# Fused retention, gated unit and expert kernel: tail outputs ahead in each pair, norm broadcasts in the gate products' banks, weight blocks begun two steps behind their request, sweep steps moved

## The chip, the cores and the metric

The kernel runs on one core of one Trainium2 chip. The metric is device time in microseconds (us): the median of timed runs of the whole program. One further execution is taken with the hardware profiler, and the trace and the profile page come from it. The engines are named as the profile names them: PE is TensorE (PEld its weight loads), DVE is VectorE, ACT is ScalarE, POOL is GpSimd, and SP (SyncE) only issues transfers here.

## The reference

Three stages follow each other: retention (attention with a decaying causal mask), a gated feed-forward unit behind a root-mean-square norm, and eight experts mixed by a normalised routing matrix.

```python
# 1: batch 4, 8 heads, 576 positions, head size 64
scores = q @ k.T / sqrt(64) * Dmat          # Dmat[i, j] = gamma[h] ** (i - j) for i >= j, else 0
x = (scores @ v)                            # 2304 tokens x 512
# 2: w_gate, w_val [512, 1536], w_out [1536, 512]
xn = x / sqrt(mean(x * x) + 1e-6) * rms_g
g = xn @ w_gate
x = (g * sigmoid(g) * (xn @ w_val)) @ w_out
# 3: w1 [8, 512, 1024], w2 [8, 1024, 512]
P = exp(x @ w_gate2 - max); 8 rounds of row and column normalisation
out = sum over e of P[:, e] * (relu(x @ w1[e]) @ w2[e])
```

## The kernel before

Products of the second and third stage are made in a 32-bit reduced format: each operand is split into a high part (a cast) and a low part (what the cast lost), and a product is three matmuls, high*high, high*low and low*high (`products`, lines L174 to L176). The order of instructions on each engine is the order in which the Python code emits them; no scheduler moves them, and each engine works strictly through its own queue.

**Retention** goes through 16 pairs (4 batches times 4 pairs of heads). A pair i has four chunks of 128 positions and a tail of 64. In loop step i the code emits `scores(i + 1)` (PE scores `sc` and the tail scores `u`, then DVE's masked product `am`), `states(i + 1)` (PE chunk states in `u`, ACT and DVE turn them into running states `block_states`, DVE makes the tail's masked scores `mt`), one call of `step_weights`, and `outputs(i)`: PE makes the four chunks' outputs in bank `o` and the tail's in a corner of `u`, DVE scales both into `acc` (L331 the chunks, L335 the tail), ACT squares the result (`sq`) and POOL sums the squares. `u`, `sc` and `o` have two buffers each, so the tail scores of pair i + 2 (L284) must wait until L335 of pair i has read `u`.

**The norm** of batch b is made in two generators. `norm_sums(b)` turns the squares into 1/rms (`ry`), the power on POOL. `norm(b)` has ACT write five diagonal tiles `dg` (L374), then PE multiply them by a matrix of ones, so that `rb` and `rbt` hold the factor of each token in all partitions (L378, L379), ACT copy these to `y` (L381, L382), and DVE scale `acc` (L387) while ACT and DVE or POOL split it into `xhi` and `xlo` (L388, L391, L393). Batch 0 is normed within retention, batches 1 to 3 beside the first three token blocks of the gated unit. `bank(name)` gives the PSUM bank for `rb`, `rbt` and the sums `ss`; after retention it comes from the pool `pac`, which also holds the four outputs `x` of a token block.

**The gated unit** makes 6 sweeps over the tokens, each with two of the 12 blocks of 128 hidden features. A sweep has five token blocks (512, 512, 512, 384, 384 tokens), and a block (`gated_block`) has five substages i = 0 to 4: gate product of feature block m = 0 (`gv`, 12 matmuls, then ACT's silu `t`, L196), value product of m = 0 (12 matmuls, then DVE's product `t` L202, ACT's cast `ghi` L203, DVE's rest `glo` L204), the same two for m = 1, and last the outputs `x` (24 matmuls: 12 with m = 0, then 12 with m = 1), which ACT copies (sweep 0, L223) or DVE adds (L225) to `acc`. PE thus starts the second 12 matmuls of `x` only when `glo` of m = 1 is there. After a substage the caller may run one `step_weights`.

**Weights** of the gated unit (36 blocks, six to a sweep) come as 64-bit numbers and are narrowed on the chip. `load_weights` requests a block into one of two raw buffers (L107, on SP). `prepare` then makes one move for each call of `step_weights`: ACT's absolute value of the raw block (L122); three operations on DVE (L124 to L126); ACT L128; DVE L130, after which the raw buffer is free and `load_weights` requests the next block at the end of the same call, and ACT's cast L142; DVE's low part L144. Two blocks are under way at a time. In the next call after a request, the first move (L122) of that new block is emitted.

Of the kernel before, what the change touches and what calls it, by code (L numbers as in the profile page):

```python
# [17 lines left out]
B, H, S, D = 4, 8, 576, 64  # L18
NP = H // 2
# [4 lines left out]
E = 8  # L24
FE = 1024
C = 128
NC = S // C
TAIL = S - NC * C
# [3 lines left out]
SWEEP = 2  # L32
# [5 lines left out]
NCONV = 2  # L38
# [12 lines left out]
def retention_glu_experts(ctx: ExitStack, tc: tile.TileContext, a, out):  # L51
# [6 lines left out]
    nc = tc.nc  # L58
# [15 lines left out]
    wg_raw = const.tile([128, KD, E], F32, name="wg_raw")  # L74
    wg = const.tile([128, KD, 2 * E], F32R, name="wg")
# [7 lines left out]
    def f32(t):  # L83
        return t.bitcast(F32)
# [7 lines left out]
    raw, raw_of, pieces, slot_of, active = {}, {}, {}, {}, {}  # L92
# [4 lines left out]
    tp = glu.enter_context(tc.tile_pool(name="tp", bufs=3, side="right"))  # L97
    nrm = glu.enter_context(tc.tile_pool(name="nrm", bufs=1, side="right"))
    raw_slots = list(range(NRAW))
    n_load, n_next, n_slot, n_done = [0], [0], [0], [0]  # L100

    def load_weights():
        while n_load[0] < len(sources) and raw_slots:
            i = n_load[0]
            n = raw_of[i] = raw_slots.pop(0)
            t = rawp.tile([128, 1024], I32, tag=f"raw{n}", name=f"raw{i}")
            nc.sync.dma_start(t, sources[i].bitcast(I32))  # L107
            raw[i] = t
            n_load[0] += 1

    def free_raw(i):
# [32 lines left out]
        nc.vector.tensor_sub(lo, x, f32(hi))  # L144
        pieces[i] = (hi, lo)

    def step_weights(load=True):
        for i in sorted(active):
            if next(active[i], True):
                del active[i]  # L150
        i = n_next[0]
        if i in raw and len(active) < NCONV:
            active[i] = prepare(i)
            next(active[i])
            n_next[0] += 1
        if load:
            load_weights()
# [86 lines left out]
    g_out = tabs.tile([128, NP, C], F32, name="g_out")  # L244
# [64 lines left out]
    def outputs(i):  # L309
        b, pr = divmod(i, NP)  # L310
        t = loaded.pop(i)
        qt, vs = t["qT"], t["vs"]
        am, mt, st, u = staged.pop(i)
        o = psa.tile([128, NC, C], F32, tag="o", name=f"o{i}")
        ot = u[:, NC + 1, :]
        for c in range(NC + 1):
            tail = c == NC
            dst = ot if tail else o[:, c, :]
            if c:
                for hs in heads:  # L320
                    cs = slice(c * C, min(S, c * C + C))
                    nc.tensor.matmul(dst[hs, :], lhsT=st[hs, c - 1, :], rhs=qt[hs, cs], start=True, stop=False)
            for h, hs in enumerate(heads):
                nc.tensor.matmul(
                    dst[hs, :],
                    lhsT=vs[hs, 2 * NC * D:] if tail else vs[:, (2 * c + h) * D:(2 * c + h + 1) * D],
                    rhs=mt[hs, :] if tail else am[:, h, c, :],
                    start=not c, stop=True,
                )
        xf = acc_d[:, pr, b * S:(b + 1) * S]  # L330
        nc.vector.tensor_mul(  # L331
            xf[:, :NC * C].rearrange("p (c i) -> p c i", c=NC), o,
            g_out[:, pr:pr + 1, :].to_broadcast([128, NC, C]),
        )
        nc.vector.tensor_mul(xf[:, NC * C:], ot, g_out[:, pr, :TAIL])  # L335
        scale_keys(i + 2)
        sq = sp.tile([128, S], F32, tag="sq", name=f"sq{i}")
        nc.scalar.activation(sq, xf, AF.Square)
        if pr:
            nc.gpsimd.tensor_add(sq, sq, squares[b])  # L340
        squares[b] = sq
# [85 lines left out]
    for i in range(B * NP):  # L427
        b, pr = divmod(i, NP)
        load_pair(i + 2, "qT", "vs")
        load_weights()  # L430
        if i == 1:
            nc.sync.dma_start(rms_g, a["rms_g"])
            nc.sync.dma_start(ident, a["ident"])
            nc.sync.dma_start(wg_raw.rearrange("p k e -> p (k e)"), a["wg"])
        scores(i + 1)
        states(i + 1)
        load_pair(i + 3, "kT", "ks")
        step_weights(load=False)
        outputs(i)
        if i in SUMS_AT:  # L440
            next(sums[i // NP - 1], None)
        if i >= 2 * NP - 1:
            next(norms[0], None)
    next(norms[1])
    nc.scalar.copy(wg[:, :, :E], wg_raw)
    nc.vector.tensor_sub(wg[:, :, E:], wg_raw, f32(wg[:, :, :E]))
    retention.close()
    psa_pools.close()
    pac = ctx.enter_context(tc.tile_pool(name="pac", bufs=4, space=PSUM, side="right"))
    ps_home[:] = pac, "ac"  # L450
    glu_ps = ExitStack()
    pmm = glu_ps.enter_context(tc.tile_pool(name="pmm", bufs=4, space=PSUM))
    xpool = ctx.enter_context(tc.tile_pool(name="xpool", bufs=1))
    sx = xpool.tile([128, 3, 2, 2, T], F32R, name="sx")
    w1_slots = [xpool.tile([128, 2, 7, 256], F32R, name="w1s0")]
# [140 lines left out]
    for s in range(NSWEEP):  # L596
        last_sweep = s == NSWEEP - 1
        for j, (t0, n) in enumerate(BLOCKS):
# [4 lines left out]
            for i in range(2 * SWEEP + 1):  # L603
                if last_sweep and last and i == 2 * SWEEP:
                    break
                if first_norms and not i:
                    next(norms[j + 1])
                next(block)
                if first_norms:
                    for _ in range((1, 1, 1, 2, 0)[i]):  # L610
# [2 lines left out]
                        next(sums[B - 1], None)  # L613
                    if i == 2 * SWEEP - 1 and j + 2 < B:
                        next(norms[j + 2])
                if i % 2 if first_norms else i != 2 * SWEEP - 1 or not s:
                    step_weights()
                if last_sweep and j and i % 2:
                    next(scored)
                if last_sweep and j == 1 and i == 2:  # L620
# [633 lines left out]
```

## Time and profile before

| | |
|---|---|
| median of 3 runs | 2050.62 us (2047.67 to 2052.09) |
| profiled execution, its own time | 2052.37 us |
| its span (first to last instruction) | 2050.6 us |
| PE busy | 2010.9 us, 98% of the span |
| DVE, ACT, POOL busy | 71%, 43%, 36% |

The span is what the trace covers; the execution's own time is 1.8 us more. Matmuls overlap each other and their ends are modelled, so PE's busy share tells little by itself: how fast it goes is read from the distance between the starts of matmuls, or from the length of a stretch with a known number of them. Retention fills the first 102 us, the gated unit goes from there to about 590 us, the experts from there to the end.

### The profile page before, as it was taken

What the parts mean: (1) busy time and instruction counts of PE and PEld (TensorE: products, weight loads), DVE (VectorE), ACT (ScalarE), POOL (GpSimd) and SP (SyncE); (2) the same over time, 40 slices, a digit from 0 to 9 for tenths busy, and PEclk for the clock granted to TensorE, in tenths of its full rate; (3) what the DMA queues carried; (4) which work ended last, traced back from release to release, by engine and by line L of the source; (5) the groups of instructions that cost most, each with busy time, mean ns of one, the idle gap of its engine ahead of it and who ended that gap; (6) DMA issues with size and microseconds to landing.
All of it is one profiled execution on the core that took longest, in us unless ns stands there. A gap on an engine that the chain in (4) does not pass through costs nothing.

```text
span 2050.6 us, 29927 instructions
## 1 busy us (share of the span) xinstructions
PE 2010.9 (98%) x11390; PEld 1857.7 (91%) x11390; DVE 1448.7 (71%) x2312; ACT 874.6 (43%) x1671; POOL 732.8 (36%) x672
## 2 busy tenths in 40 slices
PE   8989999999999999999999999999999999999998
PEld 5669789889788899989998999999999999999998
DVE  6845654643568877777786777777787777777777
ACT  4544332311354454444444444444445544444443
POOL 1210000000044445454552454545464444444443
PEclk9999999999999999999999999999999999999999
DMA  8502120200047888888888676766676676767673
GB/s 274 188 20 62 62 62 11 71 23 1 1 186 287 293 299 299 305 307 298 308 298 313 255 263 256 268 250 259 252 278 246 249 286 241 269 247 282 242 277 139
DMA packets 112687, 437.02 MB, mean 213 GB/s; under 512 B 12296, under 2 KB 30344, under 8 KB 96160
## 3 DMA queue, kind: packets, MB, share of 16 engines
q1 hardware_dynamic: 110048, 432.72, 57.9%
q10 hardware_dynamic: 2496, 2.40, 0.3%
q8 instruction: 89, 1.46, 0.3%
q14 instruction: 54, 0.44, 0.1%
HBM read 312.86 MB, written 122.21 MB: 212 GB/s over the span
## 4 chain that ended last, share of the span: by engine, by line
PE 86%; DVE 7%; ACT 3%; DMA 3%; issue 1%; POOL 1%; ACTq 0%; SPq 0%; DVEq 0%; POOLq 0%
PE pz L717 9%; PE py L717 9%; PE px L717 9%; PE qx L948 6%; PE qy L948 6%; PE qz L948 6%; PE gv L174 4%; PE gv L175 4%; PE gv L176 4%; PE y L175 4%; PE y L176 4%; PE y L174 4%; PE qz L717 3%; PE x L175 2%; PE x L176 2%; PE x L174 2%
## 5 line engine op out<-in xcount | busy, mean ns | idle before, releaser
L717 PE MATMUL py<-sx,w1s 128*128 128x384 f32 x1152 | 233.2, 337 | 2.7 <-ACT py L1041 2.5
L511 POOL TENSOR_TENSOR t<-rw 128x256 f32<-128x256 f32 x32 | 44.3, 1383 | 518.2 <-DVE sx L548 412.4
L1125 POOL TENSOR_TENSOR acc<-z,a_block 128x384 f32<-128x384 f32 x63 | 63.9, 1015 | 446.3 <-DVE z L1119 446.3
L717 PEld LDWEIGHTS py<-sx,w1s 128*128 128x128 f32 x1152 | 203.7, 189 | 7.2 <-ACT py L1041 4.2
L717 PE MATMUL px<-xhi,w1s 128*128 128x384 f32 x640 | 188.7, 335 | 0.0
L938 ACT CAST xhi<-acc 128x384 fp32r<-128x384 f32 x316 | 156.0, 514 | 69.6 <-POOL acc L1125 35.4
L942 DVE TENSOR_TENSOR xlo<-acc,xhi 128x384 fp32r<-128x384 f32 x191 | 177.4, 955 | 1.8 <-ACT xhi L938 1.8
L942 POOL TENSOR_TENSOR xlo<-acc,xhi 128x384 fp32r<-128x384 f32 x125 | 145.6, 1165 | 32.1 <-ACT xhi L938 32.0
L956 DVE TENSOR_TENSOR acc<-acc,qz 128x384 f32<-128x384 f32 x246 | 134.7, 548 | 25.6 <-PE qz L948 25.6
L202 DVE TENSOR_TENSOR t<-t,gv 128x512 f32<-128x512 f32 (+1 forms) x60 | 37.9, 632 | 131.4 <-PE gv L176 131.4
L717 PEld LDWEIGHTS px<-xhi,w1s 128*128 128x128 f32 x640 | 117.9, 188 | 0.3
L717 PE MATMUL pz<-xhi,w1s 128*128 128x384 f32 x384 | 114.1, 337 | 3.5 <-DVE z L872 2.2
L956 DVE TENSOR_TENSOR acc<-acc,qx 128x384 f32<-128x384 f32 x123 | 67.3, 547 | 70.2 <-PE qx L948 70.2
L717 PE MATMUL pz<-sx,w1s 128*128 128x384 f32 x576 | 115.7, 335 | 0.0
L717 PE MATMUL px<-xlo,w1s 128*128 128x384 f32 x320 | 107.0, 334 | 0.0
L762 DVE SCALAR_TENSOR_TENSOR acc<-y,prob,acc 128x512 f32<-128x512 f32 x144 | 101.3, 741 | 6.1 <-PE y L176 6.1
L974 ACT COPY qz<-qy 128x384 f32<-128x384 f32 x127 | 58.8, 463 | 107.0 <-PE qy L948 99.4
L176 PE MATMUL y<-xlo,xhi 128*128 128x512 f32 x264 | 103.9, 394 | 0.0
L175 PE MATMUL y<-xlo,xhi 128*128 128x512 f32 x264 | 103.7, 393 | 0.0
L174 PE MATMUL y<-xlo,xhi 128*128 128x512 f32 x264 | 102.9, 390 | 0.0
L717 PEld LDWEIGHTS pz<-sx,w1s 128*128 128x128 f32 x576 | 101.2, 188 | 0.4
L966 ACT COPY qy<-qx 128x384 f32<-128x384 f32 x127 | 58.8, 463 | 96.2 <-PE qx L948 89.9
(392 smaller groups left out, 5930.5 us busy)
## 6 DMA issues: line engine op xcount, KB each, us to landing
w1s<-w_kept SPq DMA_DIRECT2D x64, 1792.0 KB, 7.2
w_kept<-w1s SPq DMA_DIRECT2D x32, 1792.0 KB, 6.6
rw<-in_w_dram SPq DMA_DIRECT2D x64, 512.0 KB, 5.5
w_kept<-xlo SPq DMA_DIRECT2D x64, 512.0 KB, 3.5
w2s<-w_kept SPq DMA_DIRECT2D x32, 1024.0 KB, 6.9
w_extra<-w_kept SPq DMA_DIRECT2D x32, 768.0 KB, 7.6
w_kept<-xlo SPq DMA_DIRECT2D x44, 384.0 KB, 3.9
w2c<-w_kept SPq DMA_DIRECT2D x32, 512.0 KB, 7.8
```

Of the source, the lines that this page charges most:

```text
L174: nc.tensor.matmul(ps, lhsT=lh, rhs=rh, start=start, stop=False)
L175: nc.tensor.matmul(ps, lhsT=lh, rhs=rl, start=False, stop=False)
L176: nc.tensor.matmul(ps, lhsT=ll, rhs=rh, start=False, stop=stop)
L717: nc.tensor.matmul(ps, lhsT=l, rhs=r[:, k, :], start=start and k == 0 and i == 0, stop=k == 1 and i == 2, skip_group_check=True,)
L762: nc.vector.scalar_tensor_tensor(o, y_2, pe, o, ALU.mult, ALU.add)
L938: nc.scalar.copy(hi, x)
L942: (engine or nc.vector).tensor_sub(lo, x, f32(hi))
L948: nc.tensor.matmul(ps, lhsT=l, rhs=r, start=start and i == 0, stop=i == 2, skip_group_check=True)
L956: nc.vector.tensor_add(dst, dst, ps)
L966: nc.scalar.copy(y, x)
L974: nc.scalar.copy(z, y)
L1125: nc.gpsimd.tensor_add(sums[0], z[:, 0, :], h_blocks[0])
```

## The change

Four things are changed.

1. In `outputs`, the tail's matmuls come before the four chunks', and DVE scales the tail before the chunks.
2. The diagonal tiles of norm 1 (`next(norms[1])`) are emitted in retention's loop step 14, ahead of `outputs(14)`, and no longer behind the loop. After retention `bank` takes `rb`, `rbt` and the last `ss` from `pmm`, the four banks of the gate and value products, in place of `pac`. The split of the routing matrix (`wg`) moves to the last block of sweep 0.
3. A requested weight block is begun only in the third call of `step_weights` after its request (in the loop of retention still in the first).
4. In the sweeps, the calls stand after substages 0 and 1, before the emission of substage 4, and after it. Before they stood after substages 0, 1, 2 and 4. In the three blocks of sweep 0 that norm beside them the two calls stand before and after substage 4, where before they stood after substages 1 and 3.

```diff
-    n_load, n_next, n_slot, n_done = [0], [0], [0], [0]
+    n_load, n_next, n_slot, n_done, n_step, asked = [0], [0], [0], [0], [0], {}
...
-            raw[i] = t
+            raw[i], asked[i] = t, n_step[0]
...
-    def step_weights(load=True):
+    def step_weights(load=True, apart=2):
         for i in sorted(active):
             if next(active[i], True):
                 del active[i]
         i = n_next[0]
-        if i in raw and len(active) < NCONV:
+        n_step[0] += 1
+        if i in raw and len(active) < NCONV and n_step[0] - asked[i] > apart:
             active[i] = prepare(i)
...
-        for c in range(NC + 1):
+        for c in (NC, *range(NC)):
             tail = c == NC
...
         xf = acc_d[:, pr, b * S:(b + 1) * S]
+        nc.vector.tensor_mul(xf[:, NC * C:], ot, g_out[:, pr, :TAIL])
         nc.vector.tensor_mul(
             xf[:, :NC * C].rearrange("p (c i) -> p c i", c=NC), o,
             g_out[:, pr:pr + 1, :].to_broadcast([128, NC, C]),
         )
-        nc.vector.tensor_mul(xf[:, NC * C:], ot, g_out[:, pr, :TAIL])
...
-        step_weights(load=False)
+        step_weights(load=False, apart=0)
+        if i == B * NP - 2:
+            next(norms[1])
         outputs(i)
...
-    next(norms[1])
-    nc.scalar.copy(wg[:, :, :E], wg_raw)
-    nc.vector.tensor_sub(wg[:, :, E:], wg_raw, f32(wg[:, :, :E]))
     retention.close()
     psa_pools.close()
     pac = ctx.enter_context(tc.tile_pool(name="pac", bufs=4, space=PSUM, side="right"))
-    ps_home[:] = pac, "ac"
     glu_ps = ExitStack()
     pmm = glu_ps.enter_context(tc.tile_pool(name="pmm", bufs=4, space=PSUM))
+    ps_home[:] = pmm, "mm"
...
                 if first_norms and not i:
                     next(norms[j + 1])
+                if i == 2 * SWEEP:
+                    step_weights()
                 next(block)
...
-                if i % 2 if first_norms else i != 2 * SWEEP - 1 or not s:
+                if i == 2 * SWEEP or i < 2 and not first_norms:
                     step_weights()
+                if not s and last and not i:
+                    nc.scalar.copy(wg[:, :, :E], wg_raw)
+                    nc.vector.tensor_sub(wg[:, :, E:], wg_raw, f32(wg[:, :, :E]))
```

Three places show what this does to the queues. Line numbers behind the first hunks are one higher in the changed kernel (before L196, after L197). The first place is ACT in sweep 1, from the cast `ghi` of the second token block's m = 0 to the third block's first silu; `raw` is a requested weight block, `t` and `gv` carry the first token, the feature block m and, for `gv`, 0 for gate. Before:

```order
L203 CAST ghi_512_0_2170<-t_512_0_2150 128x512
L142 CAST sx<-cv_2081 128x512
L122 ACTIVATE cv_2178<-raw_2155 128x512
L196 ACTIVATE t_512_1_2195<-gv_512_1_0_2182 128x512
L122 ACTIVATE cv_2201<-raw_2180 128x512
L203 CAST ghi_512_1_2216<-t_512_1_2195 128x512
L128 ACTIVATE cv_2178<-cv_2178 128x512
L196 ACTIVATE t_1024_0_2270<-gv_1024_0_0_2257 128x512
```

and in the changed kernel:

```order
L204 CAST ghi_512_0_2148<-t_512_0_2128 128x512
L142 CAST sx<-cv_2077 128x512
L197 ACTIVATE t_512_1_2171<-gv_512_1_0_2158 128x512
L204 CAST ghi_512_1_2186<-t_512_1_2171 128x512
L122 ACTIVATE cv_2224<-raw_2133 128x512
L197 ACTIVATE t_1024_0_2239<-gv_1024_0_0_2226 128x512
L122 ACTIVATE cv_2244<-raw_2156 128x512
L204 CAST ghi_1024_0_2259<-t_1024_0_2239 128x512
```

Both reads of fresh raw blocks (L122) have moved from before `ghi` of m = 1 to behind it, and the second stands in the next token block.

The second place is ACT at the end of retention, loop steps 14 and 15 and the first copies of norm 1. Before:

```order
L128 ACTIVATE cv_1090<-cv_1090 128x512
L338 ACTIVATE sq_1256<-acc 128x576
L142 CAST wslots<-cv_1090 128x512
L128 ACTIVATE cv_1171<-cv_1171 128x512
L338 ACTIVATE sq_1283<-acc 128x576
L374 ACTIVATE dg_1286<-ident,ry_824 128x128 x5
L445 CAST wg<-wg_raw 128x4x8
L381 COPY y_1383<-rb_1379 128x512
```

and in the changed kernel:

```order
L128 ACTIVATE cv_1090<-cv_1090 128x512
L375 ACTIVATE dg_1235<-ident,ry_824 128x128 x5
L339 ACTIVATE sq_1262<-acc 128x576
L142 CAST wslots<-cv_1090 128x512
L128 ACTIVATE cv_1171<-cv_1171 128x512
L339 ACTIVATE sq_1289<-acc 128x576
L382 COPY y_1381<-rb_1377 128x512
```

The five diagonal tiles `dg` have moved ahead of both last squares, and the `wg` cast is gone from here.

The third place is DVE in a late pair of retention, from the masked product of one pair to that of the next. Before:

```order
L285 TENSOR_TENSOR am_987<-sc_986,masks 128x1024
L302 SCALAR_TENSOR_TENSOR mt_1007<-u_985,g_tail,causal_t 128x64
L304 SCALAR_TENSOR_TENSOR block_states_116<-block_states_116,g_step 128x64 x3
L130 SCALAR_TENSOR_TENSOR cv_790<-raw_753,cv_790 128x512
L331 TENSOR_TENSOR acc<-o_1020,g_out 128x512
L335 TENSOR_TENSOR acc<-u_916,g_out 128x64
```

and in the changed kernel:

```order
L286 TENSOR_TENSOR am_987<-sc_986,masks 128x1024
L303 SCALAR_TENSOR_TENSOR mt_1007<-u_985,g_tail,causal_t 128x64
L305 SCALAR_TENSOR_TENSOR block_states_116<-block_states_116,g_step 128x64 x3
L130 SCALAR_TENSOR_TENSOR cv_790<-raw_753,cv_790 128x512
L332 TENSOR_TENSOR acc<-u_916,g_out 128x64
L333 TENSOR_TENSOR acc<-o_1020,g_out 128x512
```

The read that frees `u` has moved ahead of the longer one; the rest stands as it did.

## Rows read from the trace of the kernel before

**Rows 1.** Windows of sweeps 1 to 4, first gate matmul to the next sweep's.

```profile
core 0: us, PE busy (x) PEld busy (x) DVE busy (x) ACT busy (x) POOL busy (x), PEclk, DMA share, GB/s
191.86:274.76 82.90, 78.24 (x361) 66.67 (x361) 49.59 (x87) 28.73 (x53) 0.00 (x0) 0.98 0.21 64
274.76:350.61 75.85, 74.76 (x361) 65.61 (x361) 36.59 (x62) 18.76 (x34) 0.00 (x0) 1.00 0.11 35
350.61:427.30 76.69, 75.44 (x361) 65.29 (x361) 48.68 (x86) 25.37 (x45) 0.00 (x0) 1.00 0.20 62
427.30:501.29 73.99, 73.99 (x361) 65.54 (x361) 25.13 (x41) 11.32 (x20) 0.00 (x0) 1.00 0.00 1
```

**Rows 2.** Chain that ended last, in sweep 1's last block: start, us, what.

```profile
265.96 3.62 DMA raw<-in_wout_dram
...
269.65 0.66 ACT cv L122
...
270.74 0.57 DVE glo L204
```

**Rows 3.** Timeline from the end of retention: start, us, engine, [idle before, releaser].

```profile
100.86 0.68 ACT L338 ACTIVATE sq<-acc 128x576 f32<-128x576 f32 x1 [3.48 <-DVE acc L335]
101.77 0.69 DVE L331 TENSOR_TENSOR acc<-o,g_out 128x512 f32<-128x512 f32 x1 [0.41 <-PE o L324]
101.82 0.28 PE L324 MATMUL u<-mt,vs 64*64 64x64 f32 x4
103.65 1.55 ACT L374 ACTIVATE dg<-ident,ry 128x128 f32<-128x128 f32 x5
104.96 2.07 PE L378 MATMUL rb<-dg,ones 128*128 128x512 f32 x2 [2.86 <-ACT dg L374]
```

**Rows 4.** Windows: `rb` and `rbt` of norms 1 and 2, m = 0 products behind each.

```profile
104.96:107.58 2.62, 2.62 (x4) 1.00 (x5) 0.19 (x1) 0.35 (x2) 0.26 (x1) 0.50 0.00 0
128.97:130.39 1.42, 1.42 (x5) 0.59 (x5) 0.00 (x0) 1.39 (x3) 0.00 (x0) 1.00 0.00 0
107.58:114.88 7.30, 7.30 (x25) 5.88 (x25) 0.82 (x1) 1.86 (x4) 0.00 (x0) 0.75 0.01 2
130.39:135.96 5.57, 5.57 (x25) 4.62 (x25) 0.82 (x1) 1.86 (x4) 0.00 (x0) 1.00 0.00 0
```

**Rows 5.** PE's waits from 102 to 180 us (total, times, longest), and ACT's timeline.

```profile
PE rb L378 <- ACT acc L223: 2.2, 2, 1.1
...
126.33 1.57 ACT L374 ACTIVATE dg<-ident,ry 128x128 f32<-128x128 f32 x5
```

**Rows 6.** Timeline of sweep 0's second block, around `glo` of m = 1.

```profile
139.81 1.51 POOL L391 TENSOR_TENSOR xlo<-acc,xhi 128x576 fp32r<-128x576 f32 x1 [17.23 <-ACT xhi L388]
139.61 0.42 DVE L124 TENSOR_SCALAR cv<-cv 128x512 f32<-128x512 f32 x1
139.95 1.66 DVE L125 TENSOR_SCALAR cv<-raw 128x512 int32<-128x512 int32 x1
142.98 0.68 DVE L202 TENSOR_TENSOR t<-t,gv 128x512 f32<-128x512 f32 x1
143.90 0.39 PE L176 MATMUL x<-ghi,wslots 128*128 128x512 f32 x1
145.43 0.40 PE L176 MATMUL x<-ghi,wslots 128*128 128x512 f32 x1
```

**Rows 7.** Retention: PE's waits from 20 to 102 us, a timeline row, a late window.

```profile
PE u L284 <- DVE acc L335: 3.2, 6, 0.8
...
51.12 0.33 PE L284 MATMUL u<-qT,kT 64*64 64x64 f32 x4 [0.39 <-DVE acc L335]
...
80.00:100.00 20.00, 17.94 (x250) 12.39 (x246) 18.57 (x44) 10.09 (x20) 6.68 (x4) 1.00 0.43 143
```

**Rows 8.** Windows of two idle stretches of PE in retention, with what follows each.

```profile
15.96:21.40 5.44, 4.15 (x63) 2.96 (x64) 3.15 (x9) 3.33 (x7) 0.00 (x0) 1.00 0.93 309
61.35:66.80 5.45, 4.68 (x43) 3.61 (x44) 2.21 (x7) 3.25 (x7) 1.18 (x1) 0.70 0.66 221
```

## The prediction

> **What bounds the kernel now.** I read the waits first, then the chain that ended last, then windows and timelines of the places that these named. All that the change touches lies in the first 501 us. There the end of each stage is set by PE, which always has matmuls queued, so every stretch in which PE stands, or runs at half clock, is on the path, if nothing else takes over as the limit.
>
> The gated unit's sweeps show it plainly. Sweeps 1 to 4 have the same matmuls (361 starts in each window), and they took 82.90, 75.85, 76.69 and 73.99 us [rows 1]. Sweep 4 has no weight blocks to narrow, and PE is never idle in it; 73.99 us is what a sweep costs when nothing stands in the way. The three others are above it by 8.91, 1.86 and 2.70 us, 13.5 in all. What stands in the way is seen in the chain [rows 2]: a transfer of a raw block takes 3.62 us, ACT's L122 on that block can start only then, the cast `ghi` of m = 1 is queued behind L122, and `glo` (270.74) and PE's second half of `x` come after that. The request was made after substage 1 of that block and the read stands after substage 2, in the next call. ACT is in order, so a wait for a transfer becomes a wait of PE.
>
> Around the end of retention there are three smaller places. PE ends retention at 102.10 (101.82 + 0.28) and starts `rb` of norm 1 at 104.96, since ACT makes the diagonal tiles last, from 103.65 [rows 3]. The clock is then granted at half (1.2 of 2.4 GHz): `rb` and `rbt` take 2.62 us instead of 1.42, and the first 24 gate and value matmuls 7.30 instead of 5.57 [rows 4]. And `rb` of norms 2 and 3 waits 2.2 us together for ACT to empty a bank of `x` (L223) [rows 5].
>
> **The change, part by part.**
>
> *Weight steps of the sweeps.* L122 of a block now stands at least three calls behind its request, so it does not wait for the transfer. The shortest distance is from the call before substage 4 to the call after substage 1 of the next block: 48 matmuls. 24 of them at 512 tokens take 5.57 us [rows 4], so at 384 tokens some 4.2 (three quarters, an estimate), and 48 some 8.4, against a transfer of 3.62 and, ahead of the request, three or four operations of DVE like `glo` (0.57 [rows 2]), some 2 us. No call stands between silu and `ghi` of m = 1 any more, so nothing is queued ahead of the tight one, `glo` of m = 1. The operations themselves are the same ones. Their cover is in substage 4, 24 matmuls (5.57 us) in which DVE has adds to make and ACT little; without that cover a call there would cost its longest run on DVE, the three operations L124 to L126, some 1.5 us by the 0.42 of L124 and the 0.57 of `glo` [rows 2, 6]. The price is pace: a block now takes six calls where it took four, and with two under way one is finished every three calls; 20 calls a sweep give 6.7 blocks where six are used up. The work thus reaches into sweep 4, where DVE is busy 25.13 of 73.99 us [rows 1] and has room. Bounds: nothing gained if the stalls only move, all 13.5 if they vanish. I take 13.5, because sweep 3, with nearly the DVE time of sweep 1 (48.68 and 49.59 us), is only 2.70 us above sweep 4 [rows 1]: the work itself fits beside PE.
>
> *Diagonal tiles of norm 1.* The five take 1.55 us on ACT, which idles 3.48 us ahead of its square at 100.86 [rows 3]; in their new place they fit into that idle time. `rb` then waits for DVE's last read of retention's banks, since the pools are exchanged there. DVE scales the chunks last now, 0.69 us behind PE's end (the row of 101.77) [rows 3], so `rb` starts near 102.85: 2.1 us gained. It is 2.8 if that read does not hold it, and 0 if another wait takes its place.
>
> *Clock.* The half clock followed an idle time of 2.86 us [rows 3]; 0.75 us remains. An idle stretch of 1.3 us (5.44 less 4.15) in retention left the clock at 1.00 [rows 8]. If it stays up, `rb` and the first products gain 1.20 and 1.73 us, 2.9 together; otherwise nothing.
>
> *`rb` in the gate products' banks.* The bank that it takes was read long before by DVE's L202 or ACT's silu, so the 2.2 us end, but the diagonal tiles are there only at 127.90 in the first of the two places (126.33 + 1.57) [rows 5], about when PE is ready: I count 2.1 of 2.2. In return the gate products of m = 1 wait for ACT's copies of `rb` and `rbt`; the products of m = 0 (5.57 us) lie between, and a copy is about as long as the 0.66 of L122 [rows 2], so that cost is zero; without the distance it would be about 1 us in each of three blocks.
>
> *Steps moved out of the norm blocks.* In sweep 0's second block three matmuls of `x` took 1.53 us (143.90 to 145.43) [rows 6] where 24 take 5.57, that is 0.70 for three: 0.8 us lost. DVE's L125 ran 1.66 us instead of the 0.42 of L124 beside it, with POOL's `xlo` subtraction running, and this pushed `t` to 142.98 [rows 6]. These weight operations leave that place, so I count 0.8. The Trainium skill, "SBUF — State Buffer", section "Who interferes with whom", says that a DVE operation with two SBUF inputs or in a two-port mode and a GpSimd operation that reads SBUF exclude each other for the whole instruction, the first to issue going first; L125 agrees. The norm's own scaling, which now stands there, has two SBUF inputs too. By the rule's worse order it waits for POOL until 141.32 (139.81 + 1.51), `t` begins some 0.8 us earlier than before, near 142.1, and `glo` ends three operations of 0.7 later, near 144.2, when PE could go on at 144.13: 0.1 late, and the sum would be 21.9 instead of 22.0. In the first block a similar stall (DVE waits for POOL's power) stays as it is.
>
> *Tail first.* L335 now comes ahead of L331 (0.69 [rows 3]), so 0.6 to 0.7 us sooner, and PE's six waits for it (3.2 us) [rows 7] shrink. Between 80 and 100 us DVE is busy 18.57 of 20 us [rows 7]: it is the limit there, and PE's shorter wait gains nothing. Only waits such as the 0.39 at 51.12 [rows 7] pass on. I take 0.6, with 0 and 3.2 as ends. The chunks' scaling comes a little later on DVE, and the chunk matmuls by those of the tail later on PE (0.28 [rows 3] and about as much again); both are read only by the square, which has slack, except at the very end, where it is counted above.
>
> *`wg`* (one small operation on ACT and one on DVE) goes to a block in which neither is the limit: nothing.
>
> Sum: 13.5 + 2.1 + 2.9 + 2.1 + 0.8 + 0.6 = 22.0 us. The span of 2050.6 becomes 2028.6. The profiled execution's own time, 2052.37, lies 1.75 above the median of the runs, so in the terms of that median 2050.62 - 22.0 = **2028.6 us**. The experts' part of the program is unchanged and begins earlier by the same amount.
>
> **Rivals.** (a) The clock falls all the same when the gated unit begins. For it speaks that it fell near 63.4 us after less than 1 us of idle time with matmuls of one column ahead of it (mean 0.70 in that window; 5.45 less 4.68 idle) [rows 8]; against it the 1.3 us without a fall [rows 8]. The 2.9 us are lost: 2031.5. The Trainium skill, "TensorE: Matmul & The Clock Gate", section "What's actually happening", puts it as "the default state is throttled, and activity releases the throttle", which fits a fall at such a joint.
>
> (b) The stall moves. DVE and ACT now get two calls around substage 4; if these come late to the next silu or to `acc`, PE waits there. Against it: the 2.70 us of sweep 3 with the same operations [rows 1], and the 24 matmuls of substage 4 as cover. With half of the 13.5 left: 2035.3.
>
> (c) Slower: weights come late. If the pace of one block in three calls does not suffice, the code emits the missing calls just ahead of the product that needs the block, and PE stands for request, L122 and the rest: at least 3.62 + 0.66 us [rows 2], with four more operations like `glo` some 6.6. Four such blocks eat the 22 us; with one in each of five sweeps it is 33 us, 2062. Against it: 20 calls for 18 needed, and six blocks ready before sweep 0 begins.
>
> (d) Nothing is gained, because DVE, at 49.59 of 82.90 us in sweep 1 [rows 1], or another engine is the true limit: 2050. Sweep 4's 73.99 speaks against it.
>
> **Chances.** The forecast 0.67, (a) 0.14, (b) 0.11, (c) 0.05, (d) 0.03. A difference under 0.2% (4 us) can't be told from none. Faster: 0.67 + 0.14 + 0.11 = 0.92; same 0.03; slower 0.05. The low end is the forecast with all of the waits for L335 (2.6 more), no wait of `rb` (0.7) and a little for the spread of a median: 2024.5. The high end takes in (a) and (b): 2035.5.
>
> **What would show it.** Sweeps 1 to 3 near 74 us each; no transfer ahead of L122 in the chain; `rb` of norm 1 within 1 us of the last output matmul at full clock; no wait of `rb` for L223; `x` without gaps in sweep 0's second block. The prediction is wrong if sweep 4 grows, if L122 still waits for transfers, or if the half clock returns in places where it was not.

## The result and the profile after

| | before | changed |
|---|---|---|
| median of 4 runs each, taken side by side | 2051.36 us (2047.67 to 2057.72) | 2031.56 us (2027.96 to 2033.18) |
| ratio, with its 95% interval | | 0.9898 (0.9870 to 0.9926) |
| profiled execution, its own time | 2052.37 us | 2031.48 us |
| its span | 2050.6 us | 2029.7 us |

The kernel became faster by about 20 us, where 22.0 were forecast; the time of 2031.56 us lies 3.0 above the forecast 2028.6 and inside the range. The same kernel, timed a second time in a later series, gave 2030.01 us (ratio 0.9892, 0.9873 to 0.9911).

The page of the changed kernel, its span and the first row of busy times:

```profile
span 2029.7 us, 29934 instructions
...
PE 2003.1 (99%) x11390; PEld 1856.4 (91%) x11390; DVE 1445.7 (71%) x2312; ACT 875.5 (43%) x1671; POOL 731.8 (36%) x672
```

PE's busy time fell by 7.8 us and the span by 20.9, so most of the gain is idle time of PE that is gone. Where it was is read from the same windows as before. Sweeps 1 to 4 of the changed kernel, one window each:

```profile
184.69:258.68 73.99, 73.99 (x362) 65.53 (x361) 40.46 (x71) 23.64 (x43) 0.00 (x0) 1.00 0.19 56
258.68:332.67 73.99, 73.99 (x362) 65.53 (x362) 41.41 (x73) 22.63 (x40) 0.00 (x0) 1.00 0.15 43
332.67:406.65 73.98, 73.98 (x361) 65.53 (x361) 42.77 (x76) 22.57 (x40) 0.00 (x0) 1.00 0.16 44
406.65:480.64 73.99, 73.99 (x362) 65.53 (x361) 37.27 (x64) 18.60 (x33) 0.00 (x0) 1.00 0.14 42
```

All four are now as long as sweep 4 was [rows 1], to 0.01 us, and PE is busy in all of each. DVE's work (the third number) is spread evenly, 37 to 43 us a sweep, where it was 49.59, 36.59, 48.68 and 25.13.

The joint of retention and gated unit, as a timeline (start, length, engine, what, idle time before it and its releaser):

```profile
98.85 0.97 ACT L375 ACTIVATE dg<-ident,ry 128x128 f32<-128x128 f32 x3
...
103.04 0.44 PE L325 MATMUL o<-am,vs 128*64 128x128 f32 x4
103.53 0.69 DVE L333 TENSOR_TENSOR acc<-o,g_out 128x512 f32<-128x512 f32 x1 [1.53 <-PE o L325]
...
104.36 1.10 PE L379 MATMUL rb<-dg,ones 128*128 128x512 f32 x2 [0.89 <-DVE acc L333]
```

The diagonal tiles are made 5 us ahead, and `rb` follows the last output matmul (103.04 + 0.44) after 0.88 us, released by DVE's scaling of the chunks; before it was 2.86 us, released by the tiles [rows 3]. Windows of `rb` and `rbt` of norm 1, of the first 24 gate and value products, and of `rb` and `rbt` of norm 2 (the columns are those of rows 1):

```profile
104.36:105.75 1.39, 1.39 (x4) 0.57 (x4) 0.00 (x0) 0.63 (x1) 0.68 (x1) 1.00 0.25 100
105.75:111.32 5.57, 5.57 (x25) 4.60 (x25) 0.82 (x1) 1.86 (x4) 0.73 (x1) 1.00 0.02 3
125.44:126.86 1.42, 1.42 (x7) 1.20 (x7) 0.69 (x1) 1.42 (x5) 0.00 (x0) 1.00 0.72 124
```

The clock stays at 1.00, so the first two take 1.39 and 5.57 us instead of 2.62 and 7.30 [rows 4]. PE's waits from 95 to 180 us (total, times, longest):

```profile
PE rb L379 <- DVE acc L333: 0.9, 1, 0.9
PE x L176 <- DVE glo L205: 0.2, 1, 0.2
```

No `rb` waits for ACT's reading of `x` any more [rows 5]. What the forecast did not have lies earlier, in retention. Three windows of retention in the changed kernel:

```profile
61.30:66.70 5.40, 5.40 (x68) 3.48 (x68) 2.92 (x8) 2.75 (x7) 1.18 (x1) 1.00 0.69 208
84.29:87.40 3.11, 2.65 (x33) 2.36 (x31) 2.99 (x9) 1.67 (x4) 0.55 (x1) 1.00 0.78 227
87.40:97.60 10.20, 10.13 (x94) 6.99 (x96) 8.04 (x18) 4.29 (x9) 3.37 (x2) 0.51 0.15 47
```

Before, the clock was at half for 3.4 us from 63.5 us on [rows 8]; here it is at full there, and at half from 87.7 to 97.9 us, 10.2 us with PE busy nearly throughout. Retention ends at 103.48 instead of 102.10.

Piece by piece, the two profiles against each other, and the forecast's terms for the same piece:

| piece (before, after, us) | gained | forecast |
|---|---|---|
| retention, to the end of its last matmul (102.10, 103.48) | -1.38 | 0.6 |
| from there to the first gate product (5.48, 2.27) | 3.21 | 3.3 (2.1 and 1.20) |
| sweep 0, first block (22.81, 19.69) | 3.12 | 2.8 (1.73 and half of 2.1) |
| sweep 0, second block (20.02, 17.79) | 2.23 | 1.9 (half of 2.1, and 0.8) |
| sweeps 1 to 4 (309.43, 295.95) | 13.48 | 13.5 |
| together | 20.66 | 22.0 |

The span fell by 20.9; the other 0.2 lies behind these pieces and was not followed further.

### The profile page after: what moved, and what is told of

Its sections match the earlier page's. It is cut to its first block, busy times and chain, and to the rows that moved or that the text cites. A ratio compares the mean times of both kernels' runs of the same rounds, so it can differ in the third digit from the quotient of the medians.

```text
span 2029.7 us, 29934 instructions
## 1 busy us (share of the span) xinstructions
PE 2003.1 (99%) x11390; PEld 1856.4 (91%) x11390; DVE 1445.7 (71%) x2312; ACT 875.5 (43%) x1671; POOL 731.8 (36%) x672
## 4 chain that ended last, share of the span: by engine, by line
PE 90%; DVE 6%; ACT 2%; DMA 1%; POOL 1%; issue 1%; ACTq 0%; SPq 0%; DVEq 0%; POOLq 0%
PE pz L722 9%; PE py L722 9%; PE px L722 9%; PE qx L953 6%; PE qy L953 6%; PE qz L953 6%; PE gv L175 5%; PE gv L176 5%; PE gv L177 5%; PE y L177 4%; PE y L176 4%; PE y L175 4%; PE qz L722 3%; PE x L175 2%; PE x L176 2%; PE x L177 2%
```

## The experiments

Ratios below are those of a kernel's runs to the runs of the kernel before beside it on the same chip.

**The parts alone.** The first theory was the forecast's: the terms are independent and add up. The second came from the profile after: the tail's new order drives PE's retention into the half clock and costs what the change lacks to 22. Three kernels carry one part of the change each, a fourth the whole change but the tail's order. The first is the kernel before with

```diff
-        for c in range(NC + 1):
+        for c in (NC, *range(NC)):
...
+        nc.vector.tensor_mul(xf[:, NC * C:], ot, g_out[:, pr, :TAIL])
...
-        nc.vector.tensor_mul(xf[:, NC * C:], ot, g_out[:, pr, :TAIL])
```

> The kernel before with only the tail outputs ahead in each pair. Theory 1 (the tail order gains in the pairs, and where the clock falls in retention is chance): the pair that begins at 80.5 us before begins 2 to 3 us earlier; the total is 0.5 to 3 us below before, with half clock somewhere. Theory 2 (the tail order itself brings the half clock of the last pairs): half clock again between 85 and 98 us, retention ends as late as before or later, total equal or up to 1.5 us above. Sweeps as before: 82.9, 75.9 and 76.7 us.

The second is the kernel before with the diagonal tiles of norm 1 in loop step 14, the `pmm` banks and `wg` moved, and with all calls of `step_weights` as they were:

```diff
+        if i == B * NP - 2:
+            next(norms[1])
...
-    ps_home[:] = pac, "ac"
+    ps_home[:] = pmm, "mm"
```

> The kernel before with only the diagonal tiles of norm 1 ahead and the broadcasts in the gate products' banks. Theory 1: PE's wait after retention falls from 2.9 to about 0.7 us, no half clock at the first gate products, no wait of the broadcasts for copies of x: 2.1 + 2.9 + 2.1, 6 to 7 us below before; the stall of 0.8 us in sweep 0's second block stays. Rival (the half clock comes at the joint all the same): 4 us below.

The third is the kernel before with the distance and the places of the weight steps alone:

```diff
-        if i in raw and len(active) < NCONV:
+        if i in raw and len(active) < NCONV and n_step[0] - asked[i] > apart:
...
-                if i % 2 if first_norms else i != 2 * SWEEP - 1 or not s:
+                if i == 2 * SWEEP or i < 2 and not first_norms:
```

> The kernel before with only the weight steps: begun two calls later, and the calls moved. Theory 1: sweeps 1 to 3 at 74.0 us each, 13.5 us below before, and 0.8 us in sweep 0's second block: 14.3 us below in total, with the wait and half clock behind retention as before. Rival (most of the gain needs the other parts too): sweeps above 75 us.

And the changed kernel with the tail's old order (the first diff the other way round):

> The changed kernel with the tail outputs last again. Theory 1: the late pairs begin 2 to 3 us later than in the changed kernel, and the total is 0.5 to 3 us above it, unless the clock stays up in retention by chance, which hides it. Theory 2 (the tail order brings the half clock): no half clock in the last pairs, and the total is 1 to 3 us below the changed kernel.

| kernel | median (us) | ratio | interval | change | forecast of the part |
|---|---|---|---|---|---|
| tail alone | 2053.31 | 1.0006 | 0.9993 to 1.0018 | +1.2 | -0.6 |
| norm alone | 2044.39 | 0.9966 | 0.9953 to 0.9978 | -7.0 | -7.1 (2.1, 2.9, 2.1) |
| steps alone | 2037.79 | 0.9928 | 0.9914 to 0.9942 | -14.8 | -14.3 (13.5, 0.8) |
| all but the tail's order | 2029.76 | 0.9893 | 0.9880 to 0.9907 | -22.0 | |

(The change is the ratio less one, times the 2052.24 us of the kernel before in that series.) The parts add up to -20.6 us; by the same reckoning the whole gives -20.9 in its own series, -22.2 in the later one, and -22.0 without the tail's order. So no sharing between the parts can be seen, and the tail's order gives nothing that these runs can tell from none. The sweeps of the kernel with the steps alone:

```profile
191.40:265.39 73.99, 73.99 (x362) 65.53 (x361) 40.47 (x71) 23.65 (x43) 0.00 (x0) 1.00 0.19 56
...
339.38:413.36 73.98, 73.98 (x361) 65.52 (x361) 42.79 (x76) 22.59 (x40) 0.00 (x0) 1.00 0.15 44
```

The kernel with the tail alone came out as the second theory had it: half clock from 85.2 to 95.5 us, retention up to 105.78 us, no gain. The theory falls by the kernel with the tail's old order. Two windows of its retention:

```profile
84.80:88.00 3.20, 2.66 (x32) 2.31 (x30) 3.05 (x10) 1.62 (x4) 0.49 (x1) 1.00 0.78 221
88.00:98.20 10.20, 10.19 (x94) 6.98 (x96) 8.12 (x18) 4.50 (x10) 3.42 (x2) 0.50 0.16 49
```

It has the same 10.2 us at half clock without the tail's order. That order does shorten PE's waits for DVE's scaling: 3.2 us in six waits before [rows 7], 2.5 us in five in this kernel, 0.5 us in one in the changed kernel. PE's waits of the changed kernel from 20 to 102 us:

```profile
PE u L299 <- ACT ks L267: 2.0, 3, 1.1
PE rb L379 <- DVE rv L360: 0.8, 1, 0.8
PE u L285 <- DVE acc L332: 0.5, 1, 0.5
```

and the second row of the kernel before:

```profile
PE u L298 <- ACT ks L266: 1.5, 3, 0.5
```

The wait for ACT's scaled keys `ks` grew by 0.5 us. With the unchanged 0.8 the waits listed come to 5.5 us before and to 3.3 in the changed kernel; what is left of this in the time is taken up below.

**Distance or places?** The change of the weight steps does two things at once. One kernel is the changed one with the old places of the calls, the other the changed one with the old distance:

```diff
-                if i == 2 * SWEEP:
-                    step_weights()
...
-                if i == 2 * SWEEP or i < 2 and not first_norms:
+                if i % 2 if first_norms else i != 2 * SWEEP - 1 or not s:
```

> The changed kernel with the calls back in their old places, a block still begun in the third call after its request. Theory A (the stall is the read of a raw block right behind its request, so either half of the change ends it): sweeps 1 to 3 within 0 to 2 us of 74.0 each, with short stalls of up to 0.5 us in blocks where DVE's and ACT's weight operations stand between the silu and the cast of m = 1; the 0.8 us in sweep 0's second block come back; 1 to 4 us above the changed kernel. Theory B (only the places matter): sweep 1 above 80 us again.

```diff
-    def step_weights(load=True, apart=2):
+    def step_weights(load=True, apart=0):
```

> The changed kernel with a block begun in the first call after its request, the calls in their new places. Theory A: ACT waits for the transfer behind the cast of m = 1, under the 24 matmuls of the outputs, and PE does not wait: sweeps 1 to 3 at 74.0 us, total equal to the changed kernel within 1.5 us. Theory C (only the distance matters): ACT's wait comes through to PE in substage 4 or the next silu, sweep 1 above 78 us.

Measured: 2033.74 us, ratio 0.9920 (0.9900 to 0.9940) with the distance and the old places; 2035.20 us, 0.9915 (0.9897 to 0.9932) with the places and the old distance. Sweep 1 of the one and of the other, a fence each:

```profile
187.65:261.63 73.98, 73.98 (x361) 65.55 (x361) 41.44 (x72) 23.49 (x43) 0.00 (x0) 1.00 0.14 43
```

```profile
188.84:262.90 74.06, 74.06 (x362) 65.51 (x361) 47.99 (x86) 28.43 (x52) 0.00 (x0) 1.00 0.23 64
```

Either one alone is enough for the sweeps. They do it in different ways, which ACT's waits from 150 to 500 us show. In the kernel with the distance alone no wait of L122 for a transfer is left. In the kernel with the places alone three such rows are, nearly 20 us in all, about as much as the 18.6 us (10.8 and 7.8) of the kernel before in the same view:

```profile
ACT cv L122 <- DMA raw<-in_wout_dram: 9.1, 3, 4.3
...
ACT cv L122 <- DMA raw<-in_gate_dram: 5.8, 2, 3.3
...
ACT cv L122 <- DMA raw<-in_val_dram: 5.0, 2, 2.6
```

So ACT waits as long as before and PE does not: it is what is queued behind the wait that counted. With no call between silu and `ghi` of m = 1, the cast is no longer behind such a wait.

The medians of both kernels are some 2 to 4 us above that of the changed one, though their intervals overlap with its own. In the profiles the difference is not in the sweeps: sweep 1 begins at 187.65 and 188.84 us instead of 184.69. Most of it arises in retention, which ends at 105.16 and 107.33 us, and is not the work of the part that was put back: up to 115 us all three kernels have the same instructions in the same order on each engine. The kernel with the places alone was slow at the start. Sixteen matmuls of one form between 16 and 22 us, in the changed kernel and then in this one:

```profile
L282 PE MATMUL sc<-qT,kT 64*128 64x128 f32 x16 | 1.2, 283 | 0.5 <-DMA qT<-in_qT_dram 0.5
L282 PE MATMUL sc<-qT,kT 64*128 64x128 f32 x16 | 2.1, 438 | 0.0
```

They take 438 ns instead of 283, and PE gets faster only near 23 us, although the column of the granted clock shows 1.00 there. The durations of matmuls have to be read beside that column.

With the old places the 0.8 us were expected back in sweep 0's second block. That block takes 17.75 us, as in the changed kernel (17.79); it is the third that takes 17.36 us instead of 16.47, and the first 20.12 instead of 19.69. In the third stands the pair of operations that the kernel before had in the second [rows 6]:

```profile
154.76 1.51 POOL L392 TENSOR_TENSOR xlo<-acc,xhi 128x576 fp32r<-128x576 f32 x1 [15.89 <-ACT xhi L389]
154.89 1.66 DVE L125 TENSOR_SCALAR cv<-raw 128x512 int32<-128x512 int32 x1
```

So the stall stands where L125 meets POOL's subtraction. With the places alone the three blocks take 19.71, 17.77 and 16.47 us and have none, so it takes the new places to be rid of it.

**The two places of the norm.** The changed kernel with the tiles made behind the loop again, and the changed kernel with the old banks:

```diff
-        if i == B * NP - 2:
-            next(norms[1])
...
+    next(norms[1])
```

> The changed kernel with the diagonal tiles of norm 1 behind the loop of retention again, the broadcasts still in the gate products' banks. By my sum: PE's wait ahead of the first broadcast goes from 0.9 to some 3 us, and if this wait is what brings the half clock, it follows: 2.62 us for the broadcast and 7.3 for the first 24 products, 5 us above the changed kernel in that place; the later broadcasts don't wait. Rival (the half clock there was chance): only 2.1 us.

```diff
+    ps_home[:] = pac, "ac"
...
-    ps_home[:] = pmm, "mm"
```

> The changed kernel with the broadcasts in the banks of the outputs again, the diagonal tiles early. By my sum: two waits of 1.1 us for copies of the outputs come back in sweep 0's first and second block, the start of the gated unit stays as in the changed kernel: 2.1 us above it. Rival (the broadcasts were held by the diagonal tiles, not by the bank): no difference in the first block, 0 to 1 us in the second.

One run each: 2034.06 and 2035.29 us. The joint of the kernel with the late tiles, first ACT's timeline, then PE's:

```profile
104.38 1.55 ACT L375 ACTIVATE dg<-ident,ry 128x128 f32<-128x128 f32 x5
```

```profile
105.69 1.13 PE L379 MATMUL rb<-dg,ones 128*128 128x512 f32 x2 [2.73 <-ACT dg L375]
...
107.11 0.62 PE L175 MATMUL gv<-xhi,wslots 128*128 128x512 f32 x1
```

The wait is back at 2.73 us, and the half clock with it, from 107.3 us for 3.4 us; sweep 0's first block takes 21.22 us instead of 19.69. Wait and block together cost 3.4 us, where 5 were expected: this fall came behind `rb` and was half as long as that of the kernel before (6.8 us). In the kernel with the old banks, PE's waits from 100 to 180 us:

```profile
PE rb L379 <- ACT acc L224: 2.0, 2, 1.8
PE rb L379 <- ACT cv L128: 0.9, 1, 0.9
PE x L176 <- DVE glo L205: 0.2, 1, 0.2
```

The two waits are back (2.0 us; 2.2 before [rows 5]), one of 1.8 and one of 0.2 us, and this time the clock was at half for 3.4 us from 125.7 us, behind the longer one: sweep 0's first two blocks take 2.45 and 1.48 us more than in the changed kernel. By this one profile the banks are worth 2.0 us, and 3.9 when the clock falls behind the wait.

**What keeps the clock in retention?** All twelve profiles of kernels without added work at the sums of batches 0 to 2, the kernel before among them, have a half clock of 3.4 to 10.2 us in retention behind 25 us. There are 13 such stretches. Twelve begin 1.4 to 3.4 us behind the start of the ten one-column products of the sums (`ss`) of batch 1 (near 60 us) or batch 2 (near 86 us). One, in the kernel with the tail's order alone, begins at 85.2 us, 3.7 ahead of its sums. But only 12 of the 24 sums of these two batches are followed by a fall, and those of batch 0 (from 37 to 42 us) in none of the twelve. The theory is that these products, between waits, let it fall; dense work ahead of them should keep it. The changed kernel with

```diff
+        if b < B - 1:
+            for _ in range(6):
+                nc.tensor.matmul(ss[:, 128:], lhsT=idle, rhs=idle.rearrange("p (o i) -> p o i", o=1).to_broadcast([128, 3, 128]), start=True, stop=True)
```

> The changed kernel, with six products of 128x384 bf16 put ahead of the ten one-column products of the sums of batches 0, 1 and 2 (their results are written into columns of the same bank that nobody reads). In the changed kernel's profile the half clock of 87.4 to 97.6 us begins 3.1 us after such sums begin (84.29 us), and it costs about half of its 10.2 us. Theory A (the sparse one-column products in a part of retention with little else on TensorE let the clock fall, so dense work beside them keeps it): no half clock between 20 and 103 us; the 18 added products take about 3 us (18 x 0.17, by the 384-column products of the sweeps), about 5 us come back: the gated unit begins near 104 us, and the time is about 2029.5 us, ratio near 0.989. Theory B (the fall has nothing to do with the sums: it comes by chance or with the load of the whole part): a half clock of 6 to 10 us stays in retention and the 3 us are added: the gated unit begins near 108.5 us, the time is about 2034.5 us, ratio near 0.9912.

In the same series a small remainder was tried, the 0.66 us from one `x` product to the next at 120.75 us, where a `glo` comes late:

```diff
-                    if not j and i in (1, 2):
+                    if not j and i in (1, 3):
                         next(sums[B - 1], None)
```

> The changed kernel, with the second step of batch 3's sums of squares one substage later in sweep 0's first block (two more substages of gate products between the two steps' work on VectorE). In the changed kernel's profile one product of that block waits for a correction tile glo of VectorE (product at 121.41 us, 0.23 us of idle time shown and 0.66 us from start to start where 0.23 is the rule). Theory A (the sums' work on VectorE, pulled together by the change, delays the glo): the wait goes and the first block is 0.4 us shorter, 19.3 instead of 19.69 us; the time is within 1 us of the changed kernel's 2031.5. Theory B (VectorE is full in this block whatever the order, so the wait moves): a wait of 0.2 to 1 us stands at a later glo of sweep 0's first or second block, and the first two blocks together stay at 37.5 us or grow by up to 1 us.

Then both together with three products, beside the changed kernel itself once more:

> The changed kernel with three instead of six dense products ahead of the sums of batches 0, 1 and 2 (nine in all, about 1.5 us by 0.164 us each as they took with six), and with the later second step of batch 3's sums. Theory A (dense work beside the one-column products keeps the clock, and three are enough): no half clock between 25 and 103 us; against the changed kernel 1.5 us are added, about 5 us come back and 0.7 us of the first block go: about 2027.5 us, ratio near 0.9885. Theory A' (three are too few): a half clock of 6.8 to 10.2 us begins within 4 us of the sums of batch 1 or 2, at about 65 or 89 us: about 2032 us, ratio near 0.990. Theory B (the missing fall with six was chance): half clock in retention too, and at a place not tied to the sums.

> The changed kernel once more, beside dense_three_later on one chip. Expected 2031.5 us and a ratio near 0.990 again, with the half clock of its profile in retention, 6.8 to 10.2 us long, beginning within 4 us of the sums of batch 1 or 2 (near 62 or 87 us). If the place and length come out otherwise (no fall in retention, or one elsewhere), the fall is not tied to the sums, and what the other kernel's profile shows says little.

| kernel | median (us) | ratio | interval | half clock in the profile, 0 to 130 us |
|---|---|---|---|---|
| six products | 2030.61 | 0.9897 | 0.9882 to 0.9912 | 8.9 to 22.6 |
| sums later | 2032.36 | 0.9910 | 0.9894 to 0.9927 | 60.7 to 67.5 |
| three products, sums later | 2030.04 | 0.9890 | 0.9873 to 0.9906 | 10.6 to 24.3 |
| the changed kernel again | 2030.01 | 0.9892 | 0.9873 to 0.9911 | 8.6 to 15.4, 63.2 to 66.6 |

Retention from 25 to 103 us in the kernel with six products and its start, and below the same 78 us in the kernel with three:

```profile
25.00:103.00 78.00, 75.56 (x1022) 51.98 (x1022) 66.33 (x154) 40.19 (x85) 20.91 (x14) 1.00 0.68 213
8.90:22.60 13.70, 12.55 (x122) 9.10 (x118) 5.19 (x12) 3.89 (x8) 0.00 (x0) 0.50 0.83 297
```

```profile
25.00:103.00 78.00, 75.12 (x1023) 51.60 (x1021) 66.34 (x154) 40.21 (x85) 20.91 (x14) 1.00 0.67 215
```

The clock is at 1.00 throughout, in two profiles of two, against none of twelve without the added products: the fall behind the sums goes with what PE does around them. The time did not follow. The eighteen added products cost about 1 us: the distances from the sums of batch 0 to those of batch 1, on to batch 2 and to the end of retention are 22.81, 25.11 and 15.29 us, where the two profiles of the changed kernel have 21.94, 25.01 and 15.30 in stretches without a fall. And both profiles have a half clock of 13.7 us near the start, where the program is the same as in the changed kernel; whether that is chance isn't settled by two. A slow start alone does not keep the fall away: the kernel with the places alone was slow up to 23 us and has its fall at 91.3 us.

The changed kernel's second profile has its fall at 63.2 us, 3.4 us long where 6.8 to 10.2 were expected, and ends retention at 101.92 us, 1.56 us earlier than its first. From the sums of batch 2 to the last matmul of retention, the first profile and then the second:

```profile
84.29:103.48 19.19, 18.66 (x192) 12.57 (x190) 15.00 (x37) 9.91 (x21) 5.27 (x3) 0.73 0.23 66
86.62:101.92 15.30, 14.59 (x192) 9.86 (x190) 14.60 (x37) 8.97 (x20) 4.10 (x3) 1.00 0.24 77
```

The fall of 10.2 us cost 3.9 us here. The one of 3.4 us cost 1.5 us between the sums of batches 1 and 2 (26.55 us instead of 25.01). The same program ends retention 1.6 us apart by where the clock falls.

The later step of the sums does what was expected of it. No wait for a `glo` is left, and sweep 0's first block is 0.68 us shorter, 19.01 instead of 19.69:

```profile
104.37:123.38 19.01, 19.01 (x88) 15.27 (x87) 9.83 (x19) 7.62 (x16) 4.26 (x3) 1.00 0.02 5
```

That is 0.03% of the time, and the medians can't show it. No kernel of the study is measurably faster than the changed one.

## Why the prediction was right, and where it was off

**Weight steps, 13.5 us: right.** The four sweeps give 13.48 us, and no L122 waits for a transfer from 150 to 500 us. That the sizes agree to 0.02 us holds for the one profile of before from which the term was read. A part of the 8.91 us of its sweep 1 was the clock, at half for 3.4 us from 271.7 us behind the stalls, which the forecast did not tell apart. The same sweep, with the old steps, in the kernel with the norm alone, which has no fall there:

```profile
187.26:268.55 81.29, 76.89 (x361) 65.25 (x361) 49.33 (x87) 28.73 (x53) 0.00 (x0) 1.00 0.22 65
```

In that profile sweeps 1 to 3 lie together 11.4 us above three times 73.99, where before it was 13.5; in the kernel with the tail alone, whose clock falls twice there, it is 14.4. The price in pace (the work reaching into sweep 4) appeared and cost nothing: DVE's 37.27 us there lie beside 73.99 us of PE. The reason given, that L122 must not stand close behind its request, is one of two that each suffice; the places alone, with 19.9 us of waits left on ACT, do as well.

**Diagonal tiles, 2.1 us, and clock, 2.9 us: right.** `rb` started 0.88 us behind PE's end, where 0.75 was forecast, held by the read that was named. The late tiles bring wait and half clock back together, though at 3.4 us and not 5.0. Over all profiles, the four with a wait of 2.7 to 2.9 us at this joint have a fall in that wait or within 2 us behind it, and the ten with a wait of 0.6 to 0.9 us have none. Rival (a), a fall at the start of the gated unit anyway, did not come; its time, 2031.5, is the one that was measured, but by another cause.

**Banks, 2.1 us: right.** Putting them back returns waits of 2.0 us (one run).

**Sweep 0's second block, 0.8 us: about right.** The two blocks gave 5.35 us, 0.7 more than the terms for them (4.6), and PE has no gap left in the second one's `x`. That it takes the new places, and not only the new distance, is seen from the kernel with the old places, where the same stall stands one block later (0.89 us). The worse order that was weighed there did not come. DVE's scaling and then POOL's subtraction in the changed kernel:

```profile
134.69 0.81 DVE L388 SCALAR_TENSOR_TENSOR acc<-acc,rms_g,y 128x576 f32<-128x576 f32 x1
```

```profile
134.89 1.90 POOL L392 TENSOR_TENSOR xlo<-acc,xhi 128x576 fp32r<-128x576 f32 x1 [15.94 <-ACT xhi L389]
```

DVE was first with its operation and kept its usual 0.81 us, and POOL's took 1.90 instead of 1.51 [rows 6]. The Trainium skill, "SBUF — State Buffer", section "Who interferes with whom", has the first to issue go first; the trace agrees. DVE was free from 135.50 us, 1.25 ahead of `t`, so the 0.1 us weighed for the other order did not arise.

**Tail first, 0.6 us: the step that was off.** Alone it measures +1.2 us (-1.4 to +3.7), which excludes neither 0 nor a gain of 0.6. It removes most of PE's waits for DVE's read of `u`, as stated. What that is worth is seen where the clock is full under both orders. From the sums of batch 2 to the last matmul, in the kernel with the steps alone (old order; 15.30 us with the new one, shown above):

```profile
87.42:103.13 15.71, 14.28 (x194) 9.65 (x190) 14.88 (x38) 7.88 (x16) 4.39 (x3) 1.00 0.28 86
```

Three profiles of each order lie at 15.71 to 15.72 and at 15.29 to 15.30 us: 0.42 less with the tail first. Then `rb` waits for the longer scaling and starts 0.89 us behind the last matmul; with the old order and early tiles it is 0.64. So some 0.2 us is left here, less than the runs can show. Between the sums of batches 1 and 2 there is no gain (25.01 us in the changed kernel, 24.88 with the tail's old order, no fall in either).

Behind it lies what no term had: retention ended 1.4 us later in the first profile and 0.2 us earlier in the second, by where the clock fell. The forecast took the half clock near 63 us of the one profile before [rows 8] as something that stays, while its place and length change between executions. The difference of 2.0 us between forecast and first profile in this piece is most of the 3.0 us by which the time was missed; the median of the second series is 1.4 us from the forecast.

Rivals (b) to (d) did not come: none of sweeps 1 to 4 is longer than 73.99 us, no weights are late, and PE's stalls were the bound.

## What to carry to other kernels

A stretch with the same matmuls that once runs without a stall is the price list for all its copies: the excess of the others over it was the gain, to 0.02 us in the profile from which it was read; two other profiles of the old steps, with no fall of the clock in sweep 1 and with two, give 11.4 and 14.4 us for the 13.5. A wait in an in-order queue costs only what is queued behind it; moving the waiting instruction behind the one that PE waits for did as much as ending its wait. A term below a microsecond that rests on waits of an engine which is not far from its limit, beside a clock that falls at varying places, can't be told from zero by the times of runs; profiles can tell it, from a stretch in which the clock is the same on both sides.

## What was not expected of the hardware

- PE's clock falls to half without any long idle time. In the changed kernel it fell at 87.7 us after a stretch in which PE was busy 2.65 of 3.11 us, its one wait 0.46 us, with ten one-column products in it. It stayed at half for 10.2 us although PE was busy 10.13 of 10.20 us.
- The same program has this fall near 63 us in one execution and near 88 us in another, 3.4 to 10.2 us long.
- With six products of 128x384 in bf16 ahead of the one-column ones (1.0 us in the trace, 88.74 to 89.72) the clock stayed at 1.00 from 25 to 103 us in the one profile taken, and with three in another.
- PE can run at the slow pace near the start without the column of the granted clock showing it: 438 ns instead of 283 for matmuls of one form, up to about 23 us, in one profile.
